# Linear attention, a dense layer and routed experts: the second expert's first block computed from the rows of the first seven groups

## The chip, the cores and the metric

The kernel runs on one core of one Trainium2 chip. The metric is the device time of one execution in microseconds (us). The engines are named as in the profile: PE is TensorE's products and PEld its weight loads, DVE is VectorE, ACT ScalarE, POOL GpSimd; SP is the engine that only issues DMAs, and SPq, POOLq and PEldq are the sequencers' own work.

## What is computed

```python
def reference(r, k, v, w, u, moe, moe2):             # 4 x 8 heads x 768 steps x 48
    y = linear_attention(r, k, v, w, u)              # state = w * state + k v, step by step
    x = y.transpose(0, 2, 1, 3).reshape(3072, 384)
    h = x @ moe["w_in"]                              # 384 x 2048
    x = maximum(0.01 * h, h) @ moe["w_out"]          # 2048 x 384
    do = x @ moe2["w_skip"] > 0                      # only these tokens get an expert
    e = argmax(x[do] @ moe2["w_gate"], axis=1)       # one of 8 experts for each
    g = softmax(x[do] @ moe2["w_gate"])[e]
    out = x
    out[do] += g * (maximum(x[do] @ moe2["w1"][e], 0) @ moe2["w2"][e])    # 384 x 1024 x 384
    return out
```

This is the reference cut to what matters; each expert works on its own tokens only.

## The kernel before

Tokens go through attention and the dense layer in eight groups of 384, which are three tiles of 128. Numbers are split into a high and a low float16 part (`split`: ScalarE the high one, VectorE the low one), so one product of the reference is three on TensorE. After a group's second layer (`mm2`, its end in `mm2_post`) the tiles are stored twice: to the output, and as rows of 769 numbers (both float16 parts, the value, the gate) to `xbuf` in DRAM. `routing` gives every token its expert and its place in that expert's list, and GpSimd scatters the token numbers with indirect DMAs (L592) into three lists in DRAM (`idxl`, one for each tile of a group, so that the list of an expert is the minimum over the three).

With the last group, `counts` runs beside the second layer: it takes the experts' counts, loads the lists (L605), merges them, turns them with four small products (L613) and then loads eight counts into registers of every engine (L619). Right behind stand products on zeros (`warm`, L107), which give TensorE work while it would have none.

Then come the experts in order, 0 to 7, each in blocks of 128 tokens. A block's rows are gathered from `xbuf` by an indirect DMA on GpSimd (L915, into one of seven buffers `xg`), turned by a transposing DMA in SP's queue (L920, into `xT`; for the very first block TensorE turns them, L924), multiplied with the first matrix (`hidden`, 72 products), with the second (`combine`, 24 products), added to the rows by VectorE (L955), and scattered to the output by GpSimd (L958). Blocks from the second on stand in branches on the counts. I write e1b2 for expert 1's block 2, counted from 0.

The weights of experts 2 to 7 come in 48 pieces of 384 KB each (L651, `load_expert`) into eight buffers `wb`, and `split_pieces` splits them into the places that earlier weights leave: expert 2 in `slotA` beside the last group's second layer, expert 3 in `slotB`, 4 in `slotC`, 5 in `slotD` (expert 0's place), 6 in `slotE` (expert 1's). Each first block of an expert splits up to six pieces (`PIECES`), and behind a split the next piece is loaded into the buffer. All orders are as written: every engine takes its instructions in program order, and SP issues stores, loads and transposing DMAs in one row, so that a DMA that waits there holds those behind it.

## Time and profile before

| | us |
|---|---|
| three runs | 662.92, 663.36, 666.12; median 663.36 |
| the profiled execution, its own time | 664.67 |
| its span, from the first to the last instruction | 662.8 |
| TensorE busy in the span | 615.8 (93%) |
| VectorE, ScalarE, GpSimd busy | 420.8, 256.6, 250.2 |
| mean granted clock of TensorE, share of full | 0.985 |

Nearly all of the span TensorE is at work, so the share says little; the stretches where it isn't lie at the start, around the passage from the second layer to the experts (about 511 to 526 us) and between experts. Full speed is 2.4 GHz; the lower of the two levels is 1.2 GHz, and a mean between them says what part of a stretch was spent at which.

### The profile page before, as it was taken

To read this page: it belongs to the slowest core of one execution; us is meant where nothing else is said; L and a number is where in the kernel's file an instruction comes from. 1 tells how busy PE (TensorE), PEld (TensorE's weight loads), DVE (VectorE), ACT (ScalarE), POOL (GpSimd) and SP (SyncE) were. 2 spreads that over 40 slices of the span, in tenths; PEclk is the share of its full clock that TensorE was granted. 3 is DMA by queue.
4 is the path that set the end of the run, shared out by engine and by line. 5 is a ranking of instruction groups with operands and counts; after the bars stand their busy time and mean duration, and the time that the engine had idled before them with its cause. 6 is when DMAs were issued, how large, how long until landed. Compare 5 with 4: busy or idle time off the path is not lost.

```text
span 662.8 us, 17874 instructions
## 1 busy us (share of the span) xinstructions
PE 615.8 (93%) x7253; PEld 408.8 (62%) x7253; DVE 420.8 (63%) x912; ACT 256.6 (39%) x539; POOL 250.2 (38%) x240
## 2 busy tenths in 40 slices
PE   8889988989999999999999999999999689989985
PEld 5666555656666666666666666665656557766663
DVE  7989988854289469838957933841765262463651
ACT  1226656462144236324534512531543141342530
POOL 2857764443546442633544543110141221221111
PEclk9879999999999999999999999999999889999999
DMA  8766354613726542652642530031067688087650
GB/s 271 221 190 204 90 171 137 183 65 73 168 77 150 158 146 88 158 177 69 147 146 77 113 112 23 2 85 34 1 198 237 197 216 235 24 232 205 170 126 11
DMA packets 60750, 89.25 MB, mean 135 GB/s; under 512 B 21106, under 2 KB 44624, under 8 KB 60640
## 3 DMA queue, kind: packets, MB, share of 16 engines
q1 hardware_dynamic: 57344, 82.28, 43.8%
q0 software_dynamic: 2864, 5.44, 2.9%
q8 instruction: 67, 1.10, 0.7%
q14 instruction: 43, 0.35, 0.2%
q10 hardware_dynamic: 432, 0.07, 0.1%
HBM read 69.25 MB, written 17.23 MB: 130 GB/s over the span
## 4 chain that ended last, share of the span: by engine, by line
PE 51%; DMA 14%; issue 14%; DVE 12%; POOL 5%; ACT 2%; SPq 1%; POOLq 0%; DVEq 0%; ACTq 0%
PE bank L498 8%; PE bank L499 7%; PE bank L500 7%; PE bank L470 7%; PE bank L472 6%; PE bank L471 6%; DMA out_x<-y,idx 6%; DMA xg<-xbuf,idx 5%; PE bank L399 2%; DVE wc L207 2%; DVE bank L199 2%; DVE bank L202 2%; PE bank L351 2%; PE bank L327 1%; PE bank L384 1%
## 5 line engine op out<-in xcount | busy, mean ns | idle before, releaser
L470 PE MATMUL bank<-xt,slotA 128*128 128x384 f16 x384 | 125.9, 328 | 2.4 <-DVE gg L476 2.3
L472 PE MATMUL bank<-xt,slotA 128*128 128x384 f16 x384 | 125.8, 327 | 0.0
L471 PE MATMUL bank<-xt,slotA 128*128 128x384 f16 x384 | 125.7, 327 | 0.0
L498 PE MATMUL bank<-slotB,slotC 128*128 128x393 f16 (+1 forms) x336 | 110.7, 329 | 0.0
L500 PE MATMUL bank<-slotB,slotC 128*128 128x393 f16 (+1 forms) x336 | 110.5, 329 | 0.0
L499 PE MATMUL bank<-slotB,slotC 128*128 128x393 f16 (+1 forms) x336 | 110.5, 329 | 0.0
L476 DVE TENSOR_TENSOR gg<-bank,gg 128x384 f32<-128x384 f32 x128 | 70.1, 550 | 30.6 <-ACT gg L475 29.6
L475 ACT ACTIVATE gg<-bank 128x384 f32<-128x384 f32 x128 | 61.9, 489 | 57.7 <-PE bank L472 46.0
L486 DVE TENSOR_TENSOR slotC<-gg,slotC 128x384 f16<-128x384 f32 x101 | 78.7, 782 | 0.2
L291 POOL TENSOR_TENSOR dg<-cs,diag 128x512 f32<-128x512 f32 x21 | 22.2, 1056 | 132.1 <-DVE cs L284 132.1
L485 ACT CAST slotC<-gg 128x384 f16<-128x384 f32 x112 | 56.8, 508 | 17.5 <-DVE gg L476 14.6
L526 DVE SCALAR_TENSOR_TENSOR x<-bank,x 128x384 f16<-128x384 f32 x24 | 13.2, 556 | 72.4 <-ACT x L523 72.4
L263 POOL TENSOR_TENSOR rkt<-rkt,tabs 112x512 f32<-112x512 f32 x44 | 56.8, 1315 | 0.1
L592 POOL DMA_INDIRECT idxl<-tokid,su x24 | 25.0, 1041 | 77.9 <-DVE su L589 67.8
L471 PEld LDWEIGHTS <-slotA 128*128 128x128 f16 x384 | 37.7, 98 | 25.2 <-issue 3.4
L472 PEld LDWEIGHTS <-slotA 128*128 128x128 f16 x384 | 37.7, 98 | 25.2 <-issue 0.5
L470 PEld LDWEIGHTS <-slotA 128*128 128x128 f16 x384 | 37.6, 98 | 24.0 <-issue 0.3
L500 PEld LDWEIGHTS <-slotC 128*128 128x128 f16 x336 | 32.9, 98 | 22.7
L943 ACT ACTIVATE h<-bank 128x512 f16<-128x512 f32 x28 | 16.7, 596 | 77.6 <-PE bank L939 60.7
L498 PEld LDWEIGHTS <-slotC 128*128 128x128 f16 x336 | 32.8, 98 | 21.9
L522 ACT ACTIVATE x<-bank 128x384 f16<-128x384 f32 x24 | 11.8, 492 | 88.3 <-PE bank L500 70.2
L499 PEld LDWEIGHTS <-slotC 128*128 128x128 f16 x336 | 32.9, 98 | 20.7
(190 smaller groups left out, 1310.9 us busy)
## 6 DMA issues: line engine op xcount, KB each, us to landing
wb<-in_w SPq DMA_DIRECT2D x48, 384.0 KB
nt<-in_nat SPq DMA_DIRECT2D x24, 576.0 KB
rkt<-in_rk SPq DMA_DIRECT2D x24, 448.0 KB
xbuf<-x SPq DMA_DIRECT2D x24, 384.5 KB
wst<-in_w_in SPq DMA_DIRECT2D x16, 384.0 KB
wst<-in_w_out SPq DMA_DIRECT2D x16, 384.0 KB
wst<-in_w SPq DMA_DIRECT2D x16, 384.0 KB
out_x<-x SPq DMA_DIRECT2D x24, 192.0 KB
```

The lines of the kernel that those rows point to most:

```text
L263: eng.tensor_mul(r4[:, a], r4[:, a], tab.unsqueeze(2).broadcast_to([112, NPAIR, 2, C]))
L470: pe.matmul(ph[:, :n], wh, xt[:, 0, k, t0:t0 + n], start=k == 0, stop=False)
L471: pe.matmul(ph[:, :n], wh, xt[:, 1, k, t0:t0 + n], start=False, stop=False)
L472: pe.matmul(ph[:, :n], wl, xt[:, 0, k, t0:t0 + n], start=False, stop=k == NK - 1)
L475: act.activation(gg[:, :n], ph[:, :n], AF.Copy, scale=0.01)
L476: v.tensor_max(gg[:, :n], ph[:, :n], gg[:, :n])
L485: act.copy(gT[:, 0, f, t0:t0 + n], gg[:, :n])
L486: eng.tensor_sub(gT[:, 1, f, t0:t0 + n], gg[:, :n], gT[:, 0, f, t0:t0 + n])
L498: pe.matmul(po[:, :c1 - c0], gh, w_out_s[:, 0, f, c0:c1], start=start, stop=False)
L499: pe.matmul(po[:, :c1 - c0], gh, w_out_s[:, 1, f, c0:c1], start=False, stop=False)
L500: pe.matmul(po[:, :c1 - c0], gl, w_out_s[:, 0, f, c0:c1], start=False, stop=stop)
L592: g_.indirect_dma_start(out=idxl[i], out_offset=bass.IndirectOffsetOnAxis(ap=su[:, i:i + 1], axis=0), in_=tokid[:, ti:ti + 1], in_offset=N ...
```

## The change

The rows of the first seven groups are enough for the first 128 tokens of expert 1 (`E0`), if that many of its tokens are among them. While the last group's first layer runs, their list entries are loaded (`early_list`); the smallest over the three lists gives the row numbers, a gather limited to the first 2688 rows fetches them, and a transposing DMA turns them. The block is computed right behind the second layer. Behind it stands a branch: if the seven groups held fewer than 128 tokens of expert 1 and the eighth adds some, the block is computed once more with the complete list. In its old place the block is left out, and the parity of the buffers of expert 1's other blocks is turned over. The counts, with a ninth for the branch, are loaded by one instruction on each engine. The zero products go from 15 and 40 to 8. While the last second layer runs, every split is followed by the load of a next piece, where there were two lots of four. Transposing expert 0's first rows on TensorE (`first_rows`) and its gather are parted.

```diff
@@ -42,7 +42,6 @@
 XR = 2 * DM + 1
 NW = 8
 XB = 3
-WARM = 40
 NST4 = 5
 NWC = 2
 NPAR = 8
@@ -50,7 +49,8 @@
 NB2 = 7
-WARM2 = 15
+WARM2 = 8
+E0 = 1
@@ -595,8 +595,10 @@
         yield
 
     def counts():
-        cnt = cst.tile([P, E], I32, name="cnt")
-        v.tensor_sub(cnt, run, route[:, 1, :])
+        cnt = cst.tile([P, E + 1], I32, name="cnt")
+        v.tensor_sub(cnt[:, :E], run, route[:, 1, :])
+        v.tensor_scalar_min(cnt[:, E:], cnt[:, E0:E0 + 1], P)
+        v.tensor_sub(cnt[:, E:], cnt[:, E:], steps["early"])
         yield
 
         n = NBLK * P
@@ -614,17 +616,44 @@
         steps["pt"] = pt
         yield
         v.tensor_copy(idx_t.rearrange("p j e -> p (j e)"), steps["pt"][:, :NBLK * E])
-        warm(WARM2, 2)
-        for e in range(E):
-            rv.append(nc.values_load(cnt[0:1, e:e + 1], min_val=0, max_val=NT))
-
-        warm(WARM, 2)
+        rv.extend(nc.values_load_multi_w_load_instructions(
+            cnt[0:1, :], min_val=0, max_val=NT,
+            skip_runtime_bounds_check_because="counts of ones, one for each of at most NT tokens")[1])
+        yield
+
+    def early_list():
+
+        n = rt.tile([P, 1], I32, name="early_n")
+        v.tensor_sub(n, run[:, E0:E0 + 1], route[:, 1, E0:E0 + 1])
+        v.tensor_scalar_min(n, n, P)
+        steps["early"] = n
+        lists = rt.tile([P, TPG], U32, name="early_l")
+        for i in range(TPG):
+            sp.dma_start(lists[:, i:i + 1], idxl[i][E0 * NT:E0 * NT + P, :])
+        yield
+        idx = rt.tile([P, 1], U32, name="early_i")
+        steps["early_i"] = idx
+        v.tensor_reduce(idx, lists, op=ALU.min, axis=AX.X)
+        gather(E0, 0, None, idx, NT - GT)
+        yield
+        turn_rows(E0, 0)
         yield
 
     rv = []
 
     def buf_of(e, j):
         return 3 * (e % 2) + j if j < 3 else 6
+
+    def gather(e, j, k=None, ix=None, rows=NT):
+        k = buf_of(e, j) if k is None else k
+        ix = idx_t[:, j, e:e + 1] if ix is None else ix
+        g_.indirect_dma_start(
+            out=xg_b[k], out_offset=None, in_=xbuf[:rows, :],
+            in_offset=bass.IndirectOffsetOnAxis(ap=ix, axis=0), bounds_check=rows - 1, oob_is_err=False)
+
+    def turn_rows(e, j, k=None):
+        k = buf_of(e, j) if k is None else k
+        sp.dma_start_transpose(xT_b[k], xg_b[k][:, :DM].bitcast(F16))
 
 
     def expert_views(slot):
@@ -821,6 +850,9 @@
                 if f == 12 and g > 0:
                     for i in range(TPG):
                         store_x(g - 1, i)
+                if last and f == 14:
+                    firsts = early_list()
+                    next(firsts)
         if last:
             skew(None)
             cnts = counts()
@@ -828,8 +860,8 @@
             m2p = ctx.enter_context(tc.tile_pool(name="m2p", bufs=1))
             w_b = [m2p.tile([P, 768], F32, name=f"wb{i}") for i in range(NW)]
             xg_b = [m2p.tile([P, XR], F32, name=f"xg{i}") for i in range(NB2)]
-            for t in xg_b:
-                g_.memset(t, 0.0)
+            for i in range(NB2):
+                g_.memset(xg_b[(buf_of(E0, 0) + i) % NB2], 0.0)
             idx_t = m2p.tile([P, NBLK, E], U32, name="idx")
             idx_l = m2p.tile([P, TPG], U32, name="idxl_t")
             idx_m = m2p.tile([P, 1], U32, name="idxm_t")
@@ -839,15 +871,11 @@
             later = [(e, c) for e in range(2, E) for c in range(8)]
             parts = [load_expert(*later.pop(0), w_b, NW) for _ in range(8)]
 
-            def load_pieces(n):
-                for _ in range(min(n, len(later))):
-                    parts.append(load_expert(*later.pop(0), w_b, NW))
-
-            def split_pieces(n, more=True):
+            def split_pieces(n):
                 for _ in range(min(n, len(parts))):
                     parts.pop(0)()
-                    if more:
-                        load_pieces(1)
+                    if later:
+                        parts.append(load_expert(*later.pop(0), w_b, NW))
         if g == 0:
             for i in range(TPG):
                 mm2_post(g, i, po[i], DM, False)()
@@ -877,10 +905,10 @@
                             next(rts, None)
                     if (i, q) in ((1, 0), (1, 1), (2, 1)):
                         next(cnts)
+                    if (i, q) in ((0, 2), (1, 1)):
+                        next(firsts)
                     if i < 2:
-                        split_pieces(1, False)
-                    if (i, q) in ((1, 2), (1, 3)):
-                        load_pieces(4)
+                        split_pieces(1)
                 elif g == 1:
                     if i == 0:
                         if q == 2:
@@ -910,15 +938,12 @@
     yps = bank[6:8]
 
     def fetch(e, j, k=None, ix=None):
-        k = buf_of(e, j) if k is None else k
-        ix = idx_t[:, j, e:e + 1] if ix is None else ix
-        g_.indirect_dma_start(
-            out=xg_b[k], out_offset=None, in_=xbuf,
-            in_offset=bass.IndirectOffsetOnAxis(ap=ix, axis=0), bounds_check=NT - 1, oob_is_err=False)
+        gather(e, j, k, ix)
+        turn_rows(e, j, k)
+
+    def first_rows():
+        k = buf_of(0, 0)
         xs = xg_b[k][:, :DM].bitcast(F16)
-        if e + j > 0:
-            sp.dma_start_transpose(xT_b[k], xs)
-            return
         tp = bank[0].bitcast(F16)
         for c in range(2 * NK):
             pe.transpose(tp[:, c * P:(c + 1) * P], xs[:, c * P:(c + 1) * P], ident16)
@@ -974,9 +999,24 @@
 
         tc.mark_branch_hint_location(f"e{e}b{j}", (rv[e] + (NT + 1023 - j * P)) >> 12, engines=ENGINES)
 
-    fetch(0, 0)
+    gather(0, 0)
     fetch(0, 1)
-    fetch(1, 0)
+
+
+    cuts = PIECES[0]
+    k0 = buf_of(E0, 0)
+    hidden(E0, k0, 1, 1, cuts[:2])
+    split_pieces(cuts[2])
+    combine(E0, k0, 1, steps["early_i"])
+    with tc.If(rv[E] > 0):
+        idx_f = m2p.tile([P, 1], U32, name="idxf")
+        v.tensor_scalar(idx_f, steps["early_i"], NT, 4 * NT, op0=ALU.is_lt, op1=ALU.mult)
+        v.tensor_max(idx_f, idx_f, idx_t[:, 0, E0:E0 + 1])
+        fetch(E0, 0, None, idx_f)
+        hidden(E0, k0, 0, 2)
+        combine(E0, k0, 0, idx_f)
+    warm(WARM2, 2)
+    first_rows()
     for e in range(E):
         with tc.If(rv[e] > 2 * P):
             fetch(e, 2)
@@ -985,17 +1025,21 @@
         if e + 1 < E:
             with tc.If(rv[e + 1] > P):
                 fetch(e + 1, 1)
-        announce(e, 1)
-        cuts = PIECES[e]
-        hidden(e, buf_of(e, 0), e % 2, e % 2, cuts[:2])
-        split_pieces(cuts[2])
-        combine(e, buf_of(e, 0), e % 2, idx_t[:, 0, e:e + 1], lambda: fetch_ahead(e + 2))
+        odd = 1 if e == E0 else 0
+        if e == E0:
+            fetch_ahead(e + 2)
+        else:
+            announce(e, 1)
+            cuts = PIECES[e + 1 if e < E0 else e]
+            hidden(e, buf_of(e, 0), e % 2, e % 2, cuts[:2])
+            split_pieces(cuts[2])
+            combine(e, buf_of(e, 0), e % 2, idx_t[:, 0, e:e + 1], lambda: fetch_ahead(e + 2))
         st = ExitStack()
         for j in range(1, NBLK):
             st.enter_context(tc.If(rv[e] > j * P, label=f"e{e}b{j}"))
             announce(e, j + 1)
-            hidden(e, buf_of(e, j), (e + j) % 2, 2 if j % 2 else e % 2)
-            combine(e, buf_of(e, j), (e + j) % 2, idx_t[:, j, e:e + 1])
+            hidden(e, buf_of(e, j), (e + j + odd) % 2, 2 if j % 2 else e % 2)
+            combine(e, buf_of(e, j), (e + j + odd) % 2, idx_t[:, j, e:e + 1])
         with tc.If(rv[e] > NBLK * P, label=f"e{e}b{NBLK}"):
             nb = (rv[e] + (P - 1)) // P
             k = NB2 - 1
```

Three places in the order of the engines' instructions, first SP's queue beside the last second layer. The names: `wb` weight pieces, `h<-idxl` the lists, `xbuf<-x` the rows of a tile. Before, the last of the three lists, eight pieces, and the stores of the second and third tile:

```order
L605 DMA h_6584<-idxl_60 8x512
L651 DMA wb_6551<-in_w 128x3x256
L651 DMA wb_6552<-in_w 128x3x256
L651 DMA wb_6553<-in_w 128x3x256
L651 DMA wb_6554<-in_w 128x3x256
L651 DMA wb_6555<-in_w 128x768
L651 DMA wb_6556<-in_w 128x768
L651 DMA wb_6557<-in_w 128x768
L651 DMA wb_6558<-in_w 128x768
L533 DMA xbuf<-x_6810 128x769
L534 DMA out_x<-x_6810 128x384
L533 DMA xbuf<-x_6855 128x769
```

With the change, behind the stores of the first tile and four pieces:

```order
L680 DMA wb_6562<-in_w 128x768
L607 DMA h_6590<-idxl_58 8x512
L607 DMA h_6590<-idxl_59 8x512
L607 DMA h_6591<-idxl_60 8x512
L656 DMA_TRANSPOSE xT_6586<-xg_6569 128x6x128
L680 DMA wb_6563<-in_w 128x768
L680 DMA wb_6564<-in_w 128x768
L680 DMA wb_6565<-in_w 128x768
L533 DMA xbuf<-x_6825 128x769
L534 DMA out_x<-x_6825 128x384
L533 DMA xbuf<-x_6870 128x769
```

Of the eight pieces five now stand ahead of the lists, and three behind them; between stands the transposing DMA of the early rows (`xT_6586<-xg_6569`), which waits for their gather.

Then TensorE behind the second layer's last product (L500). Before, the turning of the lists and the first products on zeros:

```order
L500 LDWEIGHTS slotC
L500 MATMUL bank_92<-slotB,slotC 128x384
L613 MATMUL bank_89<-id_140,h_6584 128x8 x4
L107 LDWEIGHTS wu
L107 MATMUL bank_90<-wu 128x256
L107 LDWEIGHTS wu
```

With the change, the weight load and first product of the early block stand there, with the one load of the counts between:

```order
L500 LDWEIGHTS slotC
L500 MATMUL bank_92<-slotB,slotC 128x384
L615 MATMUL bank_89<-id_140,h_6591 128x8 x4
L962 LDWEIGHTS slotE
L619 TENSOR_LOAD cnt
L962 MATMUL bank_90<-xT_6586,slotE 128x128
```

The eight products on zeros and the transposes of expert 0's rows now stand behind this block and the branch around its repeat.

Last, SP's queue behind the last store and the counts. Before, the transposing DMAs of e0b1 and e1b0, and in branches those of expert 0's further blocks:

```order
L920 DMA_TRANSPOSE xT_6577<-xg_6560 128x6x128
L920 DMA_TRANSPOSE xT_6579<-xg_6562 128x6x128
L981 COMPARE_AND_BRANCH
L920 DMA_TRANSPOSE xT_6578<-xg_6561 128x6x128
L983 COMPARE_AND_BRANCH
L920 DMA_TRANSPOSE xT_6582<-xg_6565 128x6x128
L983 UNCONDITIONAL_BRANCH x2
L981 UNCONDITIONAL_BRANCH
```

With the change:

```order
L656 DMA_TRANSPOSE xT_6584<-xg_6567 128x6x128
L680 DMA wb_6558<-in_w 128x3x256
L680 DMA wb_6559<-in_w 128x3x256
L680 DMA wb_6560<-in_w 128x3x256
L680 DMA wb_6561<-in_w 128x3x256
L680 DMA wb_6562<-in_w 128x768
L680 DMA wb_6563<-in_w 128x768
L1011 COMPARE_AND_BRANCH
L656 DMA_TRANSPOSE xT_6586<-xg_6569 128x6x128
```

The transposing DMA of e1b0 is gone, and six weight pieces (those behind the early block's splits) stand ahead of what follows in both: the transposing DMA of e1b1, six pieces behind expert 0's splits, then the transposing DMAs of expert 2's first block, of e1b2 and of e1b3.

## Rows read from the trace of the kernel before

**Rows 1.** Windows: busy us of each engine, PEclk, DMA share, GB/s.

```profile
494.00:502.00 8.00, 8.00 (x51) 4.83 (x50) 7.29 (x19) 6.33 (x9) 3.54 (x3) 1.00 0.96 336
...
502.00:506.00 4.00, 4.00 (x26) 2.40 (x25) 2.08 (x5) 0.87 (x2) 0.00 (x0) 1.00 0.20 24
...
511.00:518.00 7.00, 3.19 (x27) 2.71 (x27) 0.66 (x2) 2.45 (x4) 0.00 (x0) 0.94 0.98 343
...
525.70:533.80 8.10, 8.08 (x96) 6.26 (x95) 6.70 (x8) 4.47 (x7) 0.89 (x1) 1.00 0.90 151
...
533.80:547.20 13.40, 10.27 (x97) 7.38 (x98) 7.30 (x10) 5.46 (x8) 4.27 (x4) 0.87 0.97 258
...
536.00:546.00 10.00, 8.04 (x74) 5.61 (x72) 5.27 (x7) 3.85 (x6) 3.27 (x3) 0.83 0.97 307
```

**Rows 2.** Timeline of TensorE, 510.5 to 526: start, us, instruction, idle before.

```profile
510.98 1.05 PE L613 MATMUL bank<-id,h 8*128 8x8 f32 x8
...
511.97 1.81 PE L107 MATMUL bank<-wu 128*128 128x256 f16 x15
...
517.59 5.99 PE L107 MATMUL bank<-wu 128*128 128x256 f16 x40 [3.81 <-issue]
...
524.54 0.51 PE L924 MATMUL bank<-cf,xg 128*128 128x128 f16 x6 [0.96 <-DMA xg<-xbuf,idx]
...
525.70 0.22 PE L937 MATMUL bank<-xT,slotD 128*128 128x128 f16 x1 [0.65 <-DVE xT L925]
```

**Rows 3.** Chain that ended last, 495 to 526: start, us, what.

```profile
498.85 5.51 DMA idxl<-tokid,su
...
513.61 7.22 DMA out_x<-x
```

**Rows 4.** Timeline of GpSimd, 498.8 to 540.

```profile
498.85 0.97 POOL L592 DMA_INDIRECT idxl<-tokid,su  x1 [0.30 <-issue]
...
521.63 1.04 POOL L915 DMA_INDIRECT xg<-xbuf,idx  x1 [21.81 <-DMA out_x<-x]
...
537.62 1.03 POOL L915 DMA_INDIRECT xg<-xbuf,idx  x1 [0.31 <-DVE slotB L189]
```

**Rows 5.** Timeline of TensorE, 533 to 574.

```profile
533.45 0.33 PE L953 MATMUL bank<-slotD,h 128*128 128x384 f16 x1
...
534.97 0.22 PE L937 MATMUL bank<-xT,slotE 128*128 128x128 f16 x1 [1.19 <-issue]
...
540.70 0.22 PE L939 MATMUL bank<-xT,slotE 128*128 128x128 f16 x1 [1.11 <-issue]
...
547.16 0.22 PE L937 MATMUL bank<-xT,slotE 128*128 128x128 f16 x1
...
556.15 0.22 PE L937 MATMUL bank<-xT,slotE 128*128 128x128 f16 x1
...
573.43 0.23 PE L937 MATMUL bank<-xT,slotA 128*128 128x128 f16 x1 [1.27 <-issue]
```

**Rows 6.** Waits of the DMA queue's sequencer, 484 to 562: us, times, longest.

```profile
SPq L651 <- DVE slotC L486: 4.1, 1, 4.1
```

**Rows 7.** DMA issues, from the page: count and KB each.

```profile
wb<-in_w SPq DMA_DIRECT2D x48, 384.0 KB
```

**Rows 8.** Timeline of the DMA queue's sequencer, 524 to 547.

```profile
525.13 1.29 SPq L920 DMA_TRANSPOSE xT<-xg  x1
...
535.36 3.77 SPq L651 DMA_DIRECT2D wb<-in_w  x6
...
545.39 1.23 SPq L920 DMA_TRANSPOSE xT<-xg  x1
```

**Rows 9.** Source line 619, TensorE: duration ns min, median, max.

```profile
L619 PEldq TENSOR_LOAD <-cnt x8: 301/595/1003, 512.0 to 517.3; - x8
```

**Rows 10.** Timeline of VectorE, 533 to 535.

```profile
533.88 0.61 DVE L955 SCALAR_TENSOR_TENSOR y<-bank,xg 128x384 f32<-128x384 f32 x1
```

**Rows 11.** Groups by line, TensorE, 524 to 663: busy us, mean ns, idle.

```profile
L937 PE MATMUL bank<-xT,slotE 128*128 128x128 f16 x120 | 21.0, 221 | 3.2 <-issue 3.2
```

## The prediction

> **What bounds the kernel now.** Written e1b2, for example, is expert 1's block 2. First I read the windows by stage [rows 1]: at the end of the second layer TensorE is full (8.00 of 8.00 us in 494 to 502), but in 511 to 518 it works 3.19 of 7.00 us while the DMA engines are 0.98 busy. Then TensorE's own timeline there [rows 2]: the second layer's last product and the small turning products (L613) end at 512.03, what follows is 15 and then 40 products on zeros (L107), with 3.81 us of register loads between them, and the first expert's first product comes at 525.70. So 13.7 us of TensorE's time hold no work of the result. What ends that wait is read from the chain of waits [rows 3] and GpSimd's timeline [rows 4]: the last rows stored need 7.22 us from 513.61 until a gather may start, at 521.63, because two stores and eight weight loads are ahead in the same queue; the data is there at 524.5.
>
> A second dear stretch is e1b0 [rows 1, 5]: from the last product of expert 0 (533.45, ending 533.78) to e1b1 (547.16) there are 13.4 us for a block that costs 8.1 us elsewhere (525.7 to 533.8, PE busy 8.08). It has a jump (1.19 us idle), gaps inside the first layer (the longest 1.11 us), and a clock of 0.87 on the mean, that is a quarter of the time at 1.2 GHz. The DMA engines are at 0.97.
>
> The work behind 573 keeps its blocks and their order, and I let it move as one piece.
>
> **What is removed.** e1b0 leaves its place between expert 0 and e1b1: 13.4 us, less one jump, which stays, at 1.2 us [rows 5]. If all else held its time, that is 12.2 us. The 40 and 7 of the 15 zero products leave too, and seven of eight register loads per engine; both lie in the 13.7 us.
>
> **What the early block needs.** Its list loads stand on the DMA queue's own sequencer ahead of the weight loads; 3 issues of some 0.3 us. I cost them at nothing: the sequencer waits there 4.1 us for VectorE's last parts of the first layer [rows 6]. If that cover is gone, eight weight loads go out some 1 us later; they feed expert 2, which starts at 573.43 [rows 5]. VectorE's five small operations (under 0.2 us each by my estimate from neighbours) hide in the second layer, where TensorE is full.
> The early gather stands on GpSimd behind the last scatter of list entries, which starts at 498.85 and is issued within 1 us [rows 4]; so it goes out at 500.1. The weight loads now follow the splits, so five of the second eight go out by 500.3 rather than after 504.7. Before, the engines are full in 494 to 502 and then at 0.20 [rows 1]; five loads of 384 KB [rows 7] at 307 to 336 GB/s are 1.2 to 1.3 us each, 6 us, so now they are full until about 508. A gather in such a stretch took from 537.62 [rows 4] to 545.39, when the sequencer could issue the transposing DMA behind it [rows 8]: 7.8 us. A gather in quiet took 2.9, from 521.63 to the first transpose at 524.54 [rows 2, 4]. I take the former: rows at 507.9. The transposing DMA takes 1.3 us to issue [rows 8]. For its data: in 525.7 to 533.8 the engines are busy for 7.3 us with three such transfers and two gathers of 0.39 MB, 1.3 us each at 307 GB/s, which leaves 1.6 us for one. So the early operand is there at about 511.
>
> TensorE is ready at 512.03 and then loads nine counts in one instruction. Eight single loads took 3.81 us [rows 2], one 0.3 to 1.0 us [rows 9]; bounds 0.3 and 3.8, and I take 1.0, since it is one instruction. The Trainium skill ("Runtime: NRT & Kernel Launch", Instruction fetch mechanics) gives about 200 ns for each register even in bulk; nine would be 1.8 us, an estimate, and the sum would come out 0.8 us later by it; the row of eight loads gives 0.48 us each.
>
> So the early block starts at 513.0 and ends at 521.1 (8.1 us). Its six splits are the ones that expert 0's block did, on weights already loaded. Then comes the skipped repeat: a jump, 1.2 to 1.3 us of idle time [rows 5]; I take 1.2, and the upper bound is 5.5, with the gaps and the clock that followed the first of them (a rival, below). Then eight zero products at 0.12 us (15 took 1.81), 1.0 us, and from the transposes to the first product 1.16 us [rows 2]: expert 0 starts at 524.4, against 525.70. Is the gather of expert 0 ready? Behind the early operand's transfer stand three weight loads (1.18 MB) and, by the shapes in the code, 1.18 MB of stores for two tiles; the last can go out at 512.6. With the loads from 509.3, about 1.2 MB is undone then; at 343 GB/s [rows 1] 3.5 us, and I allow 2 us for the acknowledgement, an estimate, since no row parts the two: 518.1, so the gather goes out at 518.9 and is there at 521.8, 1.4 us before the transposes. Hidden.
>
> **Where the gain goes.** Expert 0 now ends at 532.5, and e1b1 could start at 533.7, e1b2 at 541.8, against 556.15: 14.4 us. But the block that went away also covered transfers. In the queue's order, six weight loads (for the early block's splits) now stand between the transposing DMAs of e0b1 and e1b1, then six more (expert 0's splits), then those of expert 2, e1b2 and e1b3. Before, only six stood ahead of e1b2. I add up the DMA work from 523.3, when the gather of e0b1, which follows the first one, is there:
> to e1b1's operand: two transposing DMAs 3.2, one gather 1.3, six loads 7.7 (0.393 MB at 307 GB/s, which is the 536 to 546 window): 12.2, so 535.5. It is needed at 533.7: a wait of 1.8 us.
> to e1b2's operand: six more loads 7.7, gathers of expert 2's and of its own rows 2.6, two transposing DMAs 3.2: 13.5, so 549.0.
> The same sum for before gives, from 525.1, five transposing DMAs 8.0, four gathers 5.2, six loads 7.7: 546.0, against an issue at 545.39 and 1.3 us of issuing [rows 8]. So the sum agrees within 2 us. A second way: before, e1b2's transposing DMA went out 10.9 us after expert 0's result (533.88 plus 0.61 [rows 10]); now the result is there at 533.1, so 544.0, and with issue and transfer 546.9. I take 548, nearer to the sum, because twelve loads are in the way and not six.
> So e1b2 starts at 548 and not at 556.15: 8.15 us gained, and 6.2 of the 14.4 are lost to the two waits. A pause of TensorE also brings the clock down: 0.87 over 13.4 us, of which 1.7 us is lost [rows 1], for gaps that sum to about 3 us. I take 1.2 us of such loss, bounds 0 and 1.7. e1b3's operand follows at about 551, needed at 556: hidden.
>
> **Sum.** 8.15 less 1.2 is 7.0 us. The profiled execution took 664.67 us (span 662.8), so 657.7; the median of the three runs is 1.3 us lower, and so the forecast is 656.4.
>
> **Rivals.**
> 1. The transfers keep up: nothing waits at e1b1 or e1b2. For it: the queue starts its loads some 11 us earlier than before, and rates of 343 GB/s occur. Against it: the sum above. Gain 14.4 us, 649.0.
> 2. The added jump costs TensorE more than an ordinary one. For it: the first block behind the jump to expert 1 lost 3.1 us in gaps and 1.2 us to the clock [rows 1, 5] just when the weight loads ran, and now weight loads run right behind the skipped repeat. Against it: expert 2's first product comes 1.27 us after the jump and without further gaps. It moves expert 0, its result and with it e1b2 by up to 4.3 us: 660.7. The same page and section of the Trainium skill say that a taken jump to a place outside the fetched window makes execution wait for a DMA; the gaps in [rows 5] agree, and whether this jump leaves the window no row shows.
> 3. Slower: the early transposing DMA blocks the queue's sequencer. It stands ahead of three weight loads and the last two stores of rows, and waits for the early gather. Let that gather land at G. The early block can start at G + 1.3 + 1.6 and expert 0 11.4 us behind it, so from G = 510 on each us moves everything. At G = 517 the gain is gone; at G = 521 the kernel is over 3 us slower, say 667. The gather would have to take 21 us, where 7.8 is the longest that I see.
> 4. The change does not do what it says: the repeat runs. Expert 1 has four blocks (of 120 products of a kind on slotE [rows 11], 24 to a block, five blocks, one is expert 6), so over 384 rows; seven groups of eight would have to hold under 128. A repeat would add a gather, a transfer and a block, 13 us: 669.
>
> **Chances.** Forecast 0.54, its own range 653 to 660; rival 1 0.15; rival 2 0.20; rival 3 0.07; rival 4 0.02; 0.02 for none of these. About 0.5%, 3.3 us, can be told from no change here: faster is under 660.0. The forecast nearly whole (0.53), rival 1 and two fifths of rival 2 (0.08) give 0.77 for faster; the rest of rival 2 and what lies between rivals 2 and 3 give 0.15; slower 0.08. The range leaves out the lower half of rival 1, the end of rival 2, and rivals 3 and 4: 650 to 661.
>
> **What would show it.** In the changed profile: TensorE's first product on slotE 0.5 to 1.5 us behind the turning products; expert 0's first product at 523 to 526; products of e1b1 near 535; an idle time of 3 to 6 us before e1b2, ended by the operand's transfer; the rest from expert 2 on as before, 6 to 8 us earlier. Wrong if the early operand comes after 513, if expert 0's block shows gaps behind the jump, or if e1b2 follows e1b1 at once.

## The result, and the profile after

The kernel after is slower by 0.7%: median 667.99 us (663.79 to 672.3, 20 runs) against 663.57 (660.83 to 667.23, 20 runs) for the kernel before, ratio 1.0072, with a 95% interval of [1.0049, 1.0094]. The forecast was 656.4. The profiled execution took 670.05 us (span 668.3, mean clock 0.976). Executions of one kernel scatter by some 4 us to either side, so a profile shows mechanisms, and only the medians rank kernels. In this part e1b2 is again expert 1's block 2; names like e5 in backticks are runs.

First the windows of after, columns as in [rows 1].

```profile
494.00:502.00 8.00, 8.00 (x51) 4.83 (x50) 6.04 (x17) 5.72 (x9) 4.58 (x4) 1.00 1.02 348
502.00:506.00 4.00, 4.00 (x27) 2.38 (x25) 2.61 (x5) 1.46 (x3) 0.00 (x0) 1.00 1.01 295
506.00:512.00 6.00, 5.00 (x31) 2.80 (x29) 0.60 (x1) 0.87 (x2) 0.00 (x0) 1.00 1.06 244
512.00:522.50 10.50, 7.26 (x81) 7.23 (x82) 4.73 (x9) 2.91 (x4) 1.97 (x2) 0.67 0.60 208
...
540.90:546.70 5.80, 5.80 (x73) 5.75 (x74) 0.69 (x1) 0.60 (x1) 0.90 (x1) 0.71 0.97 326
554.00:559.80 5.80, 5.80 (x74) 5.74 (x74) 0.69 (x1) 0.60 (x1) 0.00 (x0) 0.71 0.49 123
576.00:583.00 7.00, 6.92 (x73) 6.92 (x74) 1.65 (x2) 1.33 (x2) 1.04 (x1) 0.57 0.21 59
```

The DMA engines, 0.20 busy in 502 to 506 before, are now full from 494 to 512, with the five loads put ahead and the early rows. TensorE pays four times with a low clock (0.67, 0.71, 0.71, 0.57), each time behind an idle stretch. Where it was idle stands in its timeline (L615 are the list products, L962 a first layer's first product):

```profile
512.94 1.12 PE L615 MATMUL bank<-id,h 8*128 8x8 f32 x8 [1.94 <-DVE x L525]
516.36 0.27 PE L962 MATMUL bank<-xT,slotE 128*128 128x128 f16 x1 [2.30 <-issue]
...
529.02 0.22 PE L962 MATMUL bank<-xT,slotD 128*128 128x128 f16 x1 [0.65 <-DVE xT L950]
...
540.90 0.23 PE L962 MATMUL bank<-xT,slotE 128*128 128x128 f16 x1 [3.80 <-DMA xT<-xg]
...
553.98 0.22 PE L962 MATMUL bank<-xT,slotE 128*128 128x128 f16 x1 [3.36 <-DMA xT<-xg]
...
576.08 0.28 PE L962 MATMUL bank<-xT,slotA 128*128 128x128 f16 x1 [4.48 <-DVE slotC L189]
```

The early block starts at 516.36 (forecast 513.0), expert 0 at 529.02 (524.4; before 525.70 [rows 2]), e1b1 at 540.90 (535.5), e1b2 at 553.98 (548), expert 2 at 576.08, where before it was 573.43 [rows 5]. The first two delays have their causes in VectorE's timeline (the merge of the lists) and in the load of the counts (tile `cnt`, duration in ns):

```profile
511.40 0.68 DVE L610 TENSOR_TENSOR h<-h 8x512 f32<-8x512 uint32 x1 [6.70 <-DMA h<-idxl]
```

```profile
L619 PEldq TENSOR_LOAD <-cnt x1: 3305/3305/3305, 513.0 to 513.0; - x1
```

The merge waited 6.70 us for the lists. Their loads were issued when they were before (from 501.85, before from 501.55), so what is late is their transfers, which share the engines with the weight loads. And TensorE's one load took 3.3 us. Then GpSimd and the DMA queue's sequencer (columns as in [rows 4] and [rows 8]):

```profile
499.61 1.04 POOL L650 DMA_INDIRECT xg<-xbuf,early_i  x1 [0.30 <-issue]
...
528.04 1.03 POOL L983 DMA_INDIRECT out_x<-y,early_i  x1 [5.51 <-DVEq L1011]
530.68 1.23 POOL L650 DMA_INDIRECT xg<-xbuf,idx  x1 [1.61 <-DMA idxl<-tokid,su]
...
540.78 1.02 POOL L650 DMA_INDIRECT xg<-xbuf,idx  x1 [0.31 <-issue]
```

```profile
523.65 1.23 SPq L656 DMA_TRANSPOSE xT<-xg  x1
524.98 4.37 SPq L680 DMA_DIRECT2D wb<-in_w  x6
536.96 1.75 SPq L656 DMA_TRANSPOSE xT<-xg  x1
539.21 3.86 SPq L680 DMA_DIRECT2D wb<-in_w  x6
543.18 11.40 SPq L656 DMA_TRANSPOSE xT<-xg  x3
```

e1b1's rows (530.68) go out behind the early block's scatter (528.04), e1b2's (540.78) behind expert 0's; between the transposing DMAs stand twice six weight loads. Last, the branch that ends expert 1, of two the second (ns: shortest, median, longest):

```profile
L1043 PEldq COMPARE_BRANCH  x2: 245/1809/3373, 569.2 to 571.8; - x2
```

The balance to TensorE's last product, 660.46 against 655.26, is +5.2 us: expert 0 starts 3.3 later; from its end to e1b1 it is 3.80 instead of 13.38, so -9.6; from the start of e1b1 to that of e1b2 13.08 instead of 8.99, +4.1; the blocks e1b2 and e1b3 +1.6 (clock); the jump to expert 2 +3.2; expert 2's block +2.8 (first layer 7.00 instead of 4.19, clock); the rest -0.3.

### The profile page after: what moved, and what is told of

Same layout as the page of the kernel before. It is cut to its first block, busy times and chain, and to the rows that moved or that the text cites. A ratio compares the mean times of both kernels' runs of the same rounds, so it can differ in the third digit from the quotient of the medians.

```text
span 668.3 us, 17749 instructions
## 1 busy us (share of the span) xinstructions
PE 614.2 (92%) x7206; PEld 410.3 (61%) x7206; DVE 421.0 (63%) x917; ACT 256.1 (38%) x539; POOL 250.0 (37%) x240
## 5 line engine op out<-in xcount | busy, mean ns | idle before, releaser
L500 PE MATMUL bank<-slotB,slotC 128*128 128x393 f16 (+1 forms) x336 | 110.5, 329 | 0.0
L475 ACT ACTIVATE gg<-bank 128x384 f32<-128x384 f32 x128 | 61.9, 489 | 58.0 <-PE bank L472 45.5
L485 ACT CAST slotC<-gg 128x384 f16<-128x384 f32 x112 | 56.8, 508 | 17.5 <-DVE gg L476 17.5
L526 DVE SCALAR_TENSOR_TENSOR x<-bank,x 128x384 f16<-128x384 f32 x24 | 13.2, 555 | 66.5 <-ACT x L523 65.3
L969 DVE SCALAR_TENSOR_TENSOR h<-bank,h 128x512 f16<-128x512 f32 x28 | 19.3, 690 | 52.4 <-ACT h L968 46.8
L500 PEld LDWEIGHTS <-slotC 128*128 128x128 f16 x336 | 32.9, 98 | 22.8
L498 PEld LDWEIGHTS <-slotC 128*128 128x128 f16 x336 | 32.8, 98 | 21.9
```

The costliest lines, as they stand in the source:

```text
L475: act.activation(gg[:, :n], ph[:, :n], AF.Copy, scale=0.01)
L485: act.copy(gT[:, 0, f, t0:t0 + n], gg[:, :n])
L498: pe.matmul(po[:, :c1 - c0], gh, w_out_s[:, 0, f, c0:c1], start=start, stop=False)
L500: pe.matmul(po[:, :c1 - c0], gl, w_out_s[:, 0, f, c0:c1], start=False, stop=stop)
```

## The experiments

The table gives each run's ratio to the kernel before on its own chip, and from its profile TensorE's first products of the early block, of expert 0 and of expert 2 and its last product, in us behind the end of the second layer.

| run | ratio, 95% | early | e0 | e2 | end |
|---|---|---|---|---|---|
| before | 1 | - | 14.6 | 62.4 | 144.2 |
| `e12` before again | - | - | 16.1 | 61.6 | 143.0 |
| `e2` before, 42 dead products | 1.0008 [0.9971, 1.0045] | - | 14.0 | 59.2 | 140.6 |
| `e13` before, 41 dead products | 0.9986 [0.996, 1.0012] | - | 13.0 | 56.2 | 137.3 |
| `e7` before, one count load | 1.0013 [0.9981, 1.0044] | - | 13.2 | 57.9 | 139.5 |
| `e8` and loads behind splits | 0.9948 [0.9918, 0.9978] | - | 10.3 | 54.3 | 139.3 |
| `e16` the same again | 0.9961 [0.9935, 0.9987] | - | 10.8 | 54.7 | 136.0 |
| after | 1.0072 [1.0049, 1.0094] | 5.4 | 18.0 | 65.1 | 149.5 |
| `e1` 172 dead instructions | 1.0011 [0.9976, 1.0046] | 2.5 | 15.3 | 61.9 | 144.0 |
| `e11` 2 dead instructions | 1.0045 [1.0017, 1.0073] | 2.7 | 15.9 | 60.3 | 142.6 |
| `e3` loads in two lots | 1.0065 [1.0035, 1.0094] | 0.9 | 17.1 | 64.6 | 147.8 |
| `e4` counts first | 1.0059 [1.0028, 1.0091] | 3.7 | 17.5 | 64.4 | 151.6 |
| `e5` rows ahead | 1.0028 [0.9999, 1.0057] | 3.5 | 16.6 | 63.1 | 143.8 |
| `e6` `e5`, `e4` and 172 dead | 1.0036 [1.0004, 1.0067] | 2.9 | 16.0 | 60.5 | 143.7 |
| `e9` `e5`, no early splits | 1.0029 [0.9998, 1.0061] | 3.6 | 16.9 | 52.0 | 143.0 |
| `e10` `e9`, counts first | 1.0015 [0.998, 1.0049] | 3.2 | 15.1 | 52.1 | 142.0 |
| `e14` loads on ScalarE's queue | 1.022 [1.0185, 1.0255] | 4.7 | 17.7 | 58.8 | 153.1 |
| `e15` `e14`, rows ahead | 1.0186 [1.0134, 1.0237] | 3.1 | 19.3 | 58.4 | 152.2 |
| `e17` `e11`, half loads | 0.9881 [0.9836, 0.9927] | 0.9 | 11.5 | 51.3 | 133.4 |
| `e18` before, half loads | 0.993 [0.9907, 0.9953] | - | 12.3 | 59.9 | 140.2 |

### The jump out of expert 1: e1, e2, e11, e13

Dead products, which no execution reaches, shift the code behind them.

```diff
         combine(E0, k0, 0, idx_f)       # e1 (after; inside the repeat that is skipped)
+        warm(86, 2)                     # e11: warm(1, 2)
```

```diff
                 combine(e, k, e % 2, idx_m)   # e2 (before; expert 0's loop past block 4)
+                if e == 0:
+                    warm(42, 2)               # e13: warm(41, 2)
```

> The changed kernel with 86 products on zeros more inside the branch of the repeat, which is never taken; they are never executed, but all code of TensorE behind them stands 172 instructions further on. Theory of the code's place: the 4.48 us of idle time ahead of expert 2's first product come from where the jump out of expert 1 and its target lie; here they lie as in the kernel before, so the idle time falls to 1.3 us, expert 2's first layer runs at full clock (4.2 us and not 7.0), and the time falls by about 6 us, to some 662. Rival, that TensorE waits there for VectorE's split, as the profile's releaser says: nothing changes, 668.

> The kernel before with 42 products on zeros more in the loop for blocks from the fifth on of expert 0, which is never entered; code from expert 1 on stands 84 instructions further on, so that the jump out of expert 1 lies as in the changed kernel. Theory of the code's place: the idle time ahead of expert 2 grows from 1.27 to about 4.5 us, expert 2's first layer runs at the lower clock, and the time rises by about 6 us, to some 669.5. Rival (a wait for VectorE that only the changed kernel has): 663.5, idle time 1.3 us.

> Kernel after with one zero product (2 TensorE instructions) in the repeat that is never entered, so that everything behind it lies 2 instructions later. In the kernel after and the two runs that cost as much, the jump out of expert 1 lands on the seventh instruction (offset 6) of a 256-instruction stretch of TensorE's code; in the run with rows ahead, where it cost 1.28 us, on the ninth (offset 8). Theory (the place of the target in that stretch decides): the jump falls from 4.5 to 1.3 us and expert 2's first layer from 7.0 to 4.2, the waits of e1b1 and e1b2 stay: -6 us in the profile, 662 to 665 in the median. Rival (what came before the jump decides, such as low clock and waits): jump still 4.4 us or more, no change.

> Kernel before with 41 zero products in expert 0's never entered repeat (the run with 42 had the jump out of expert 1 at 1.33 us and the same median as before). Expert 1's jump lands on TensorE instruction 60 of a stretch of 256, counted from the program's start; it landed on 61 in the three runs where it cost 4.4 to 4.7 us, on 62 or 63 in four where it cost 1.3, with the jump 221 instructions ahead in each. Theory (code is fetched in pieces whose border lies between 61 and 62; a target that is among the last of the jump's own piece finds the next piece not yet fetched): the jump costs about 4.4 us and expert 2's first layer runs at the low clock, so +6 us in the profile against the run with 42. If unprofiled executions pay it as well, the median is 0.6 to 0.9% above before; if it is mostly a matter of profiled executions, within 0.3%. Rival (61 alone, or what precedes the jump): 1.3 us, no change.

The offsets in `e11`'s expectation are those of expert 0's jump, which I had taken for expert 1's; expert 1's lands on instruction 61 of a stretch of 256 in after, `e3` and `e4`, on 63 in `e11`, on 62 in `e2` and `e5`, on 60 in `e13`, on 234 in before. So `e2` and `e13`, which were to bring the cost into the kernel before, land beside 61, and no run of that kernel lands on it. The idle time in front of expert 2 was 4.48, 4.67 and 4.37 us in the three with 61; 1.26 to 1.34 in all other profiles of the table. In `e11`, two instructions further:

```profile
568.92 0.23 PE L962 MATMUL bank<-xT,slotA 128*128 128x128 f16 x1 [1.27 <-DVEq L1044]
```

So two instructions take away 3.2 us of idle time and 2.8 us of low clock, while the wait before e1b2 stays (4.99 there). That fits the place of the code, as far as one profile of each shows. My theory of why, a border between 61 and 62, falls with `e13`: 60 cost 1.27. In the three costly profiles an instruction fetch (queue q8, 16 KB) starts 1.06 to 1.09 us behind expert 1's last product; in before, `e1`, `e5`, `e6` and `e8` one comes ahead of that product's end. This is a clue and no proof: in `e2`, `e11` and `e17` one starts 0.06 to 0.64 us behind it, and the idle time is 1.27 to 1.33 all the same. Nor is the cost in the medians what the profile says: 6 us would be 0.9%, and `e11` against after is 1.0045 to 1.0072, a difference of 0.3% with an uncertainty of 0.4%. `e1` gained 0.6% (uncertainty 0.4%), but its 172 instructions move all later jumps.

### The start: e3, e4

```diff
-                        split_pieces(1)           # e3
+                        split_pieces(1, False)
+                    if (i, q) in ((1, 2), (1, 3)):
+                        load_pieces(4)
```

```diff
+        rv.extend(...)            # e4: the load of all counts
         ...                       # the list products
-        rv.extend(...)
```

> The changed kernel with the weight loads beside the last second layer as before: two lots of four behind the lists, none behind the splits. Theory that the late lists and the late early operand come from the five loads put ahead of them: the lists are merged by 507 (511.4 before this edit), the products that turn them start at 511.0 and not 512.9, the early block starts about 2 us earlier; but eight loads now stand behind the early rows' transfer and ahead of the stores, so the gather of expert 0's rows goes out 1 to 3 us later, hidden by the early block. Time 1 to 3 us lower, 665 to 667. Rival, that the load of the counts alone sets the start: within 1 us of 668.

> The changed kernel with the load of the counts ahead of the products that turn the lists, not behind them. The early block started at 516.4, after 1.9 us of waiting for the lists and then 3.3 us of the load. Theory that these two add up only because of their order: the load runs while the lists are awaited, the early block starts at 514.1 to 515.4, the pause is shorter and less of it is computed at 1.2 GHz: time 1 to 4 us lower, 664 to 667. Rival, that the early rows' operand is what is late: start unchanged, 668.

In `e3` the lists were in time: list products without a wait, count load 1.04 us, the early block at 509.86 and at full clock. But expert 0's rows were then gathered at 521.51, behind the stores that stand behind the same loads, TensorE idled 5.39 us and ran at the low clock: 17.1 instead of 18.0. In `e4` the count load hid (1.04 us), the wait for the lists stayed (2.31), and most of the earlier start went to the clock (first layer 6.96). Neither median gains (1.0065 and 1.0059, against 1.0072): each edit takes a wait away, and the next wait or the clock takes its place.

### The waits in expert 1: e5, e6, e9, e10

```diff
     fetch(0, 1)                            # e5, e6, e9, e10, e15
+    with tc.If(rv[1] > P):
+        fetch(1, 1)
+        with tc.If(rv[1] > 2 * P):
+            fetch(1, 2)                    # and these leave their old places
...
-PIECES = 6 * [(2, 1, 3)] + [(1, 1, 2), (0, 0, 0)]                                 # e9, e10
+PIECES = [(0, 0, 0), (2, 1, 3)] + 4 * [(2, 2, 3)] + [(2, 1, 3), (0, 0, 0)]
```

> Kernel after, with the gathers and transposing DMAs of expert 1's second and third block issued right behind those of expert 0's second block, ahead of the early block, instead of in expert 0's and expert 1's places. Theory (these two transfers are what e1b1 and e1b2 wait for, because GpSimd issues them only behind the early block's scatter and e0's y): the waits of 3.80 and 3.36 us fall to under 0.5 each, and with them the low clock of the two first layers (5.8 instead of 4.2 each): together -9 us at the end of e1b3 (571.6 to about 562.5), and the kernel comes under the kernel before, near 659 to 661, whatever the jump into expert 2 costs. Rival A (the DMA queues are full: what comes earlier here comes later elsewhere): the weight loads behind the early block's splits are issued behind the two transposing DMAs, e0's splits then wait for weights, and e1b1 and e1b2 start only 3 to 5 us earlier in sum. Rival B (only the wait moves): no change within 2 us.

> As the run with rows ahead, with the count load ahead of the list products too, and with 86 zero products in the repeat that is never entered (code behind it lies 172 instructions later). If the three costs of the kernel after stand beside each other (waits of e1b1 and e1b2 with their clock -9, jump out of expert 1 with its clock -6, early block's start -0.7), this is 668 - 15 = about 653; if the gains hide one another, 657 to 661; if the jump's cost comes back with the other moved instructions, about 659.

> As the run with rows ahead, and no weight piece is split (and so none loaded) in the early block; expert 0's block splits 6 as before, the later experts 7, 7, 7, 7 and 6 instead of 6, 6, 6, 6 and 4. Theory (the run with rows ahead failed because three transposing DMAs stand on SyncE's queue from 526.3 to 535.4 ahead of the loads that e0's splits wait for): e0's six splits now find pieces that were loaded during the second layer, so the stall of 7.35 us in e0's second layer goes, e1b1 starts behind e0 at about 536 to 537 (546.57 with rows ahead, 540.90 in the kernel after), e1b2 and e1b3 follow without a wait, and expert 2 starts at 561 to 564 (573.7 with rows ahead, 576.1 after): the kernel ends 9 to 12 us before the run with rows ahead, under the kernel before by 1 to 1.5%. Rival (another wait takes the place: e1b1 then waits for its transposing DMA, the third in the queue, until about 538, or the later experts stall for their splits): gain of 3 to 6 us, about even with the kernel before.

> The same with the count load ahead of the list products. Theory: another 0.5 to 1.5 us earlier, as far as the early block's low clock leaves it. Rival: no difference, since e0 waits for its gathered rows, not for the early block.

In `e5` the two waits are gone, and expert 0's second layer waits 7.36 us instead, since ScalarE's split ahead of its activation waits for a weight load; the sequencer's rows say why:

```profile
526.29 9.11 SPq L656 DMA_TRANSPOSE xT<-xg  x3
535.72 11.64 SPq L680 DMA_DIRECT2D wb<-in_w  x12
```

Rival A holds: three transposing DMAs stand in front of twelve loads. `e6` adds no gain. With the early splits gone (`e9`), experts 0 and 1 run as the theory said: e1b1 at 536.92, expert 2 at 562.62. But TensorE's timeline goes on:

```profile
562.62 0.23 PE L962 MATMUL bank<-xT,slotA 128*128 128x128 f16 x1 [1.27 <-DVEq L1048]
...
578.94 0.50 PE L976 MATMUL bank<-slotB,h 128*128 128x384 f16 x1 [2.74 <-ACT h L968]
...
620.72 0.50 PE L976 MATMUL bank<-slotD,h 128*128 128x384 f16 x1 [4.14 <-ACT h L968]
```

and the waits of ScalarE in 526 to 640 (us in total, times, longest) name the cause:

```profile
ACT slotE L188 <- DMA wb<-in_w: 7.9, 2, 7.5
ACT slotC L188 <- DMA wb<-in_w: 6.2, 1, 6.2
```

Expert 2 starts 11 us earlier than in `e5`, and the splits beside experts 3 and 5 find no weights. The stretch from expert 2 to the end takes 91.0 us, 80.7 in `e5` and 81.8 in before. Nearly all is given back; `e10` repeats it. The rival, that the later experts stall for their splits, holds beside the theory. This lead was bought by putting six splits, and the loads behind them, later. Leads of other kinds are kept, most of them whole: in `e13` and `e16` expert 2 starts 6 to 8 us earlier than in before, and the rest takes 81.1 and 81.3 us (`e17` 82.1, `e8` 85.0).

### The parts without the move: e7, e8, e16, e12

```diff
-        for e in range(E):                                        # e7, e8
-            rv.append(nc.values_load(cnt[0:1, e:e + 1], ...))
+        rv.extend(nc.values_load_multi_w_load_instructions(cnt[0:1, :], ...)[1])
...
-                        split_pieces(1, False)                    # e8 only
-                    if (i, q) in ((1, 2), (1, 3)):
-                        load_pieces(4)
+                        split_pieces(1)
```

> Kernel before, with the eight count loads of each engine replaced by the one load of all counts, nothing else. Theory (TensorE's loads lie beside the gather that the transposes wait for): no change, 663.8 within 0.7; TensorE's one load takes 1.0 to 3.3 us. Rival (GpSimd and SyncE come to the gather sooner, so that e0 starts sooner): -1 us. The jump into expert 2 stands 7 loads earlier in the code; if its cost hangs on the place it may change from 1.3 to about 4.5.

> Kernel before, with the one count load and with each weight load issued right behind the split that frees its buffer (not 4 and 4 behind the seventh and eighth split); expert 1's first block in its old place. Theory (the loads in front of the lists and of the last rows delay these): list products wait for lists as in the kernel after (about 1.5 to 2 us beyond the end of the second layer), but since e0's gather comes at about 520 either way the end stays within 1 us of the kernel before; e1's first block, whose splits waited for weights (13.4 us in the kernel before), gains 1 to 3 us from loads that come earlier. So 661 to 664. Rival (loads delay the last rows): e0 starts later, 665 to 667.

> The kernel with one count load and loads behind their splits, first block of expert 1 in its old place, a second time. If its first result was not chance (0.9948 of the kernel before, 0.9918 to 0.9978), again 0.993 to 0.998.

> The kernel before itself, for a second profile. If the profile on which the forecast rests was typical, GpSimd issues the gather of e0's rows 10.6 us behind the end of the second layer, and expert 1's first block takes 12.2 us from its start to the next block's. If that was chance: 6 to 9 us, and 8 to 10 us, as in the three runs that come from the kernel before.

One count load changes nothing that can be measured. Together with loads behind splits it makes the kernel 0.4 to 0.5% faster, twice: the last rows' stores no longer stand behind eight loads, and expert 0 starts first of all full-size variants. GpSimd and TensorE in `e8`:

```profile
517.39 1.04 POOL L910 DMA_INDIRECT xg<-xbuf,idx  x1 [17.18 <-DMA xbuf<-x]
```

```profile
521.58 0.22 PE L932 MATMUL bank<-xT,slotD 128*128 128x128 f16 x1 [0.65 <-DVE xT L920]
...
565.59 0.23 PE L932 MATMUL bank<-xT,slotA 128*128 128x128 f16 x1 [1.27 <-issue]
```

This beats both kernels: what after adds to these two edits, the move and the fewer zero products, costs 1.1 to 1.2% (1.0072 against 0.9948 and 0.9961), or 0.5 to 1.0% with the code placed as in `e1` and `e11`. The second profile of before, `e12`, shows expert 0's rows as late as the first (their gather 11.9 us behind the second layer, 10.6 in the first), but e1b0 otherwise: from expert 0's end to e1b1 it took 13.4 us in the first, 13.1 in `e18`, 11.9 in `e2`, and 9.1 to 9.2 in `e12`, `e7`, `e8`, `e13` and `e16`.

### Queue or transfers: e14, e15, e17, e18

```diff
-                    if later:                                       # e14, e15
-                        parts.append(load_expert(*later.pop(0), w_b, NW))
+                    ...          # behind the next split, and on ScalarE's queue:
+                        parts.append(load_expert(*held.pop(0), w_b, NW, act))
```

```diff
+        if isinstance(pool, list) and (e, c) >= (3, 0):             # e17 (on e11), e18 (on before)
+            sp.dma_start(t[:, :384].rearrange("p (a b) -> p a b", a=n), src[:, :, :384 // n])
+        else:
             sp.dma_start(t3, src)
```

> Kernel after (its code shifted so that expert 1's jump lands on 62, the cheap place) with the weight loads from the early block on issued by ScalarE, each behind the split that follows the one that freed its buffer; SyncE's queue then holds only the transposing DMAs. Theory (SyncE's queue is the limit): the transposing DMAs of e1b1 and e1b2 are issued as soon as their gathers land, so the waits in front of them fall from 3.8 and 3.4 us to about 1 or less (the gathers of e1b2 still wait for e0's y), and later loads are not held by transposing DMAs (they were, for 5 to 30 us): the time from the second layer's end to the end of the kernel falls from 142.6 (the run with two instructions) to about 135, median about 653. Rival A (transfers or GpSimd's order are the limit): no change, 660 to 663. Rival B (ScalarE now waits for VectorE before it can issue, and the activations behind it are late): +2 to +5 us.

> The same with expert 1's second and third rows gathered and turned ahead of the early block, as in the run with rows ahead; splits as in the kernel after. Theory: e0's splits no longer wait behind three transposing DMAs (7.35 us there), e1b1 starts behind e0 at about 536, expert 2 at about 561 to 563, and since all 6 splits are made in the early block and 6 in e0's, nothing is given back at experts 3 and 5: 131 to 134 us from the second layer's end to the end, median 648 to 652, below every kernel so far. Rival A (the transfers are the limit): e0's splits wait as long for loads that share the engines with the turned rows: within 2 us of the run with rows ahead (0.3% over before).

> Kernel after with two instructions of shift (cheap jump), and every weight load from expert 3 on brings only half of its piece (192 KB instead of 384 KB; the same number of loads, splits and products, the other half of the buffer is old data, so the experts 3 to 7 are computed with wrong weights). Theory (the transfers are the limit): the list products come right behind the second layer, the waits ahead of e1b1 and e1b2 (1.4 and 5.0 us) shrink to 1 to 2 in sum, expert 2 starts 50 to 54 us behind the second layer's end (60.3 with full loads) and the kernel ends 130 to 134 us behind it (142.6): median 650 to 654. Rival (GpSimd's and SyncE's order is the limit: the gathers still stand behind scatters and the transposing DMAs behind loads): expert 2 at 57 us or later, median 657 to 662.

> Kernel before with the same halved loads, the control. If the transfers are light, what is left between the second layer's end and e0 is the way of the last rows (stores, gather, transposes), 10 to 12 us, and e1b0 runs without gaps: expert 2 at 54 to 56 us, end at 137 to 139, median 656 to 658. Then the move is worth 4 to 8 us with light transfers (theory), against -3 us with full ones. If the kernel before gains as much as the kernel after or more, the transfers are not what takes the gain of the move.

On ScalarE's queue, each issued one split later, the loads make the kernel slower by 2%, all of it behind expert 2's first product (from there 94.3 us in `e14`, 82.2 in `e11`). The wait before e1b2 is gone in `e14`, so SyncE's order did set that one; the wait before e1b1 stays (4.12 us), while the engines are full and move little (window as above):

```profile
536.00:542.00 6.00, 1.88 (x13) 0.93 (x11) 2.80 (x4) 1.22 (x2) 2.03 (x2) 0.91 1.09 203
```

Later ScalarE's activations are late, as rival B had it (waits of 4.70 and 6.88 us before the second layers of experts 3 and 5). Now e1b2 in `e11`, and then `e17`, which is `e11` with half loads, on TensorE:

```profile
549.83 0.26 PE L962 MATMUL bank<-xT,slotE 128*128 128x128 f16 x1 [4.99 <-DMA xT<-xg]
```

```profile
512.91 1.05 PE L615 MATMUL bank<-id,h 8*128 8x8 f32 x8
513.90 0.23 PE L965 MATMUL bank<-xT,slotE 128*128 128x128 f16 x1
...
535.88 0.23 PE L965 MATMUL bank<-xT,slotE 128*128 128x128 f16 x1 [1.97 <-DMA xT<-xg]
...
547.00 0.22 PE L965 MATMUL bank<-xT,slotE 128*128 128x128 f16 x1 [1.40 <-DMA xT<-xg]
```

No wait for lists, no low clock in the early block, 3.4 us of waits in expert 1 instead of 6.4 in `e11` (1.36 and 4.99), expert 2 at 51.3 us. The medians are 656.3 and 659.47 us, 0.9881 and 0.993 of before: after against before is now 0.995, with an uncertainty of 0.5%, where `e11` was 1.0045. So lighter transfers bring the change 0.9% (uncertainty 0.6%); that it is then the faster kernel is at the edge of the uncertainty. The control missed what was expected of it, 656 to 658: e1b0's place took 13.1 us in its profile, with gaps as in before, though the loads were halved. The size is under the theory's 4 to 8 us, and since loads behind splits alone brought 0.4 to 0.5%, what the move itself is worth with light loads may be nothing: the control that parts the two, half loads in `e8`, was not run.

## Why the prediction was wrong

**What bounds the kernel.** The idle 13.7 us were there, and the early block ran in them. Two steps failed in the profile: "expert 0 starts at 524.4" (it started at 529.02, later than in before), and "I let it move as one piece" (it met a dear jump). In the medians a third came to them, the 12.2 us for e1b0's place. From expert 0's first product to expert 2's TensorE took as long for four blocks, 47.06 us, as before for five, 47.73 [rows 2, 5]; the windows of after, the whole and three parts of it (columns as in [rows 1]):

```profile
529.02:576.08 47.06, 35.43 (x384) 28.55 (x384) 15.22 (x20) 9.28 (x14) 9.31 (x10) 0.92 0.56 154
537.10:540.90 3.80, 0.00 (x1) 0.01 (x1) 0.77 (x2) 0.00 (x0) 2.15 (x3) 1.00 0.59 103
550.60:554.00 3.40, 0.04 (x2) 0.02 (x1) 0.62 (x1) 0.00 (x0) 1.48 (x2) 1.00 1.23 204
560.00:566.00 6.00, 6.00 (x68) 4.58 (x67) 1.31 (x2) 0.47 (x1) 1.00 (x1) 1.00 0.00 0
```

Of the 47.06 us four blocks at full clock are 32.2, idle time 11.6 (3.80, 3.36, 4.48) and low clock 3.3. The DMA engines are 0.56 busy over it: 0.59 while e1b1 is awaited, full while e1b2 is, and at rest from 560 on. So it is not the whole amount of the transfers that sets this stretch but when each can go: the gathers behind the scatters on GpSimd (with the gathers ahead, in `e5`, both waits are gone and one for weights comes instead), the transposing DMA of e1b2 behind the loads (in `e14` its wait is gone). The variants of before take 43 to 48 us with five blocks, and `e8`'s 44.0 are TensorE's own time but for two jumps (2.5) and some clock (1.6); `e1` and `e11`, without the dear jump, take 46.6 and 44.4 with four. `e9` does four in 35.1, and pays later.

I had added up DMA work, and not followed GpSimd's order. e1b1 came 5.4 us later than forecast (540.90 against 535.5), the early block's end 5.3 (526.43 against 521.1), and e1b1's gather stands behind that block's scatter; that the one makes the other is argued from these rows, not tested by itself.

**Where the forecast's error lies.** TensorE's last product was forecast, in the profile, 7.0 us before 655.26, and ended at 660.46, so 12.2 us off: 4.6 for expert 0's start, 2.1 for more low clock in e1b1 and e1b2 than I had allowed, 6.0 for the jump to expert 2 and the clock behind it, -0.2 for the waits and -0.3 for the rest.

**"12.2 us" for e1b0's place** comes from the dearest of eight profiles of before and its variants; in five it is some 8 us (9.1 less the jump). So in most of these executions some 4 us less were to be won. I read as a property of the place gaps that three of eight show; what makes them stays open.

**List loads "at nothing".** For the early list this held: the weight loads behind its three loads start at 487.98, before at 488.00. What had no term is the complete lists, which come late behind the five loads put ahead: "TensorE is ready at 512.03" became 514.06. The list products waited 1.9 us in after, 0 in `e3` and `e17`. The early operand itself was in time; in `e9` TensorE waited 1.13 us for it, until 514.19.

**Count load 1.0 us** (bounds 0.3 to 3.8): 3.3 in after and 3.4 in `e14`, 1.03 to 1.07 in nine of the twelve runs that load nine counts: the right value for most executions, and the upper part of the bounds in this one. The Trainium skill ("Runtime: NRT & Kernel Launch", Instruction fetch mechanics) by its 200 ns for each register gives 1.8 us for nine, an estimate; the runs lie on both sides of it.

**Early block 8.1 us.** 10.1, since it follows 4.2 us of idle time and runs at a low clock at first; I had allowed for no clock loss there. **The skipped repeat** cost almost nothing (0.15 us ahead of the zero products, where I had 1.2), so rival 2 did not come where I put it.

**The two waits.** The size was right: 7.2 us of idle time, the jump included, against 7.4 (1.2, 1.8 and 4.4). The mechanism, transposing DMAs behind weight loads, was right for e1b2; for e1b1 it was not the whole, since 4.12 us stay in `e14`, where no loads stand in that queue. They came on top of an expert 0 that starts 4.6 us late, and the clock loss behind them was 3.3 us against 1.2.

**"I let it move as one piece".** Failed at the jump into expert 2, which cost 6 us more in the profile (4.48 us idle instead of 1.27, then 7.00 instead of 4.19), by the code's place as far as `e11` shows; behind it the rest held. Nor does a lead up to expert 2 always last: `e9` and `e10` gave theirs back, since the later experts wait for weights; `e13` and `e16` kept theirs.

Rivals 3 and 4 did not come: the early transposing DMA was issued at 507.55, the repeat never ran. What came on the slower side was the one thing I had put no rival on, that the lists behind more loads, the count load and the clock delay the early block, and with it expert 0. The parts of the chance for "faster" add up to 0.76, not 0.77.

Open: why landing on instruction 61 costs 4.4 us, how much of it unprofiled executions pay, what makes the gaps in e1b0's place, and what the move is worth with light loads beyond the two other edits.

## What to carry to other kernels

Idle time on the bounding engine is worth filling only if the work that is pulled in leaves no hole where it stood: for each operand that then comes sooner, follow what brings it, in the order of the queues: behind which scatter its gather stands, and behind which loads its transposing DMA. A sum of DMA work isn't enough; here the engines were 0.59 busy while TensorE waited for e1b1. A stall in one profile, such as the gaps in e1b0's place, should be seen in a second one before its removal is booked as a gain. Of a change of several parts run each alone: here the side edit, loads as soon as a buffer is free, made the better kernel.

## What I had not expected of the hardware

In after each of TensorE's pauses of 3.36 to 4.48 us (the first in two parts, 1.94 and 2.30) cost about 1.6 to 2.8 us again: first layers of 5.8 to 7.0 us instead of 4.19 at a granted clock of 0.57 to 0.71, that is for the greater part at 1.2 GHz.

The same load of nine counts took 990 ns on ScalarE, 1085 on GpSimd, 2022 on SyncE, 2573 on VectorE and 3305 on TensorE in one execution.

A jump over 221 instructions cost TensorE 4.4 to 4.7 us of idle time in the three profiles in which its target lay on instruction 61 of a stretch of 256, and 1.3 in those where it lay on 60, 62 or 63. The Trainium skill ("Runtime: NRT & Kernel Launch", Instruction fetch mechanics) says that a taken branch outside the fetched window waits for a DMA; the fetch about 1.1 us behind expert 1's end in the three costly profiles agrees, those in `e2`, `e11` and `e17`, sooner and at no such cost, leave it open, and no run here shows where that window ends.
